# Two of three split-weight tiles get an interleaved layout in a sigmoid-attention and two-FFN kernel

## The chip, the cores and the metric

The kernel runs on one core of a Trainium2 chip. The metric is the device time of one execution in microseconds (us), lower is better. Within the core five engines run side by side and wait for one another through semaphores: TensorE (PE, matrix products; the profile lists its weight loads apart as PEld), VectorE (DVE), ScalarE (ACT), GpSimd (POOL) and SyncE (SP). The last two only issue transfers here.

## The reference

Sigmoid attention over 4 batches, 12 heads, 448 positions and 64 head dimensions is followed by two feed-forward blocks over the 1792 tokens (model width 768, inner width 2048).

```python
scores = scale * np.matmul(q, k.transpose(0, 1, 3, 2)) - np.log(S)
attn = 1.0 / (1.0 + np.exp(-scores))
x = np.matmul(attn, v)              # then to (B * S, H * D)
h = x @ w_in;  g = np.maximum(h, 0) ** 2;       x = g @ w_out      # first block
h = x @ w_in2; g = h / (1 + np.exp(-1.702 * h)); x = g @ w_out2    # second block
```

q, k, v and the output are 32-bit floats. The weights are 64-bit floats and reach the chip as plain bits, which is why the kernel has a step that decodes them.

## The kernel before

**Stages.** Attention comes first. Then come eight stages of the feed-forward blocks (STAGES, line 56): each of the two blocks has its two products, each for two pairs of batches. One product of a stage is done by Strassen's scheme in Winograd's form, so a stage multiplies seven combinations of weight blocks (P1 to P7) with seven combinations of activations, each in NF = 8 steps. One such step is a *unit*; a stage has 56 units and the kernel 448.

**A unit.** Products are done with each 32-bit operand split in a high part, rounded to the type fp32r, and a low part, the rest. A unit covers three chunks of 128 weight columns. For each chunk `product` (line 475) issues three matmuls into one PSUM bank: high weights by high activations (L486), high by low (L487), low by high (L488). Every matmul first loads its 128x128 weights into the array and then streams 448 columns of activations. A unit is nine matmuls, and the 448 units are 4032.

**The weights' way.** `prep` (line 205) decodes the weights, forms the sums that the scheme needs, and stores the blocks to memory. `plan_weights` (line 460) then brings them back for two units at a time (a *pair*; 224 pairs): two transfers fill a tile of LD (four of them, W = 384 columns for each of the two units), ACT writes the high parts to the split tile SL (L470, recorded under the helper's line L164), and DVE subtracts to get the low parts (L472, recorded under L167). There are NSLOT = 3 split tiles, used in turn: pair q has tile q mod 3. ACT may overwrite a tile once the last unit of the pair three before has been multiplied; a unit may start once its pair's low parts are there.

```python
109    SL = [cpool.tile([P, 2, 2, W], F32R, name=f"s{n}") for n in range(NSLOT)]
479            sh, lo = sl[:, 0, unit % 2], sl[:, 1, unit % 2]
484                cols = slice(c * P, (c + 1) * P)
486                nc.tensor.matmul(o, sh[:, cols], t[:, 0, k], start=start, stop=False, skip_group_check=True)
```

So in every partition a split tile has four runs of 384 words, in this order: the high parts of the pair's first unit, those of its second, the low parts of the first, those of the second. Within a run the three chunks of 128 columns follow each other.

**Order.** Instructions are issued in an order that `settle` and `run` work out ahead from planned costs (`act`, `dve`, `move`), which the change leaves as they are. SP issues the LD loads, POOL those of `prep`. The activations' split tiles T, which the matmuls stream, are made by ACT and DVE in `Operand` (line 412) in the same way.

Of the kernel before, what the change touches and what calls it, by code (L numbers as in the profile page):

```python
# [9 lines left out]
F32R = mybir.dt.float32r  # L10
# [8 lines left out]
P = 128  # L19
# [17 lines left out]
NK = 3  # L37
NF = 8
W = NK * P
UNITS = 7 * NF  # L40
NLOAD = 4
NSLOT = 3
# [48 lines left out]
def sigmoid_attention_two_ffn(ctx: ExitStack, tc: tile.TileContext, qk, v, w, outT):  # L91
# [3 lines left out]
    nc = tc.nc  # L95

    def f(ap):
        return ap.bitcast(F32)
# [7 lines left out]
    cpool = ctx.enter_context(tc.tile_pool(name="cpool", bufs=1))  # L106
    X = [[cpool.tile([P, NK, S], F32, name=f"xq{i}{j}") for j in range(2)] for i in range(2)]
    LD = [cpool.tile([P, 2, W], F32, name=f"ld{n}") for n in range(NLOAD)]
    SL = [cpool.tile([P, 2, 2, W], F32R, name=f"s{n}") for n in range(NSLOT)]
    T = []  # L110
    for n in range(NT):
        skip = 0 if n else APART
        t = cpool.tile([P, skip + 2 * NK * S], F32R, name=f"t{n}")
# [34 lines left out]
    def act(fn, n, keys=(), after=(), extra=0.0, **kw):  # L148
        return Node("act", fn, 0.115 + extra + 0.833e-3 * n, keys, after, 0.105, **kw)

    def dve(fn, n, keys=(), after=(), each=1.041e-3, **kw):
        return Node("dve", fn, 0.1 + each * n, keys, after, 0.085, **kw)

    def move(eng, out, in_, size, keys=(), after=(), **kw):

        def go():
            eng.dma_start(out() if callable(out) else out, in_() if callable(in_) else in_)

        n = Node("sp" if eng is nc.sync else "pool", go, 0.45 if eng is nc.sync else 0.55, keys, after, DMA_US + size / 250e3, **kw)
        n.size = size  # L160
        return n

    def activation(out, in_, fn=AF.Copy, **kw):
        nc.scalar.activation(out, in_, fn, **kw)  # L164

    def tt(out, in0, in1, op):
        nc.vector.tensor_tensor(out=out, in0=in0, in1=in1, op=op)  # L167
# [6 lines left out]
    def att_order():  # L174
        for u in range(NHP // 2 + 1):
            if u:
                yield from (("V", hp, c) for hp in (2 * u - 2, 2 * u - 1) for c in range(NFULL))
                yield ("VL", u - 1, 0)
            if u < NHP // 2:
                todo = [("S", hp, c) for hp in (2 * u, 2 * u + 1) for c in range(NFULL)]  # L180
                todo.insert(0 if u else NFULL, ("SL", u, 0))
                yield from todo
# [3 lines left out]
    def make_steps():  # L186
        kind = "L"
        us = {"S": SCORES_US, "V": VALUES_US, "VL": LEFT_US, "SL": LEFT_US}
        for key in att_order():
            new = "L" if key[0] in ("VL", "SL") else key[0]  # L190
            t = us["V" if key in WHOLE else key[0]]
# [61 lines left out]
    def load_qk(hp):  # L253
        if hp > 1:
            n = move(nc.sync, RQ[hp % 4], qk[hp], P * ROW * 4, (), [pe.get(("SL", (hp - 4) // 2, 0)), split.get(hp - 4)], part=0)
            rq_load[hp] = n, n
# [29 lines left out]
    def next_two():  # L286
        turn[0] += 1
        b = 2 * (turn[0] % 4)
        return b, mem["ps"][:, b : b + 2]
# [28 lines left out]
    def scores_left(u):  # L318
        b, ps = next_two()
        step = pe["SL", u, 0]  # L320

# [138 lines left out]
    def plan_weights():  # L460
        for q in range(len(STAGES) * UNITS // 2):
            m, io, _ = STAGES[2 * q // UNITS]
            us = [ORDER[io][(2 * q + i) % UNITS] for i in range(2)]
            t, sl = LD[q % NLOAD], SL[q % NSLOT]
            ld = ("LD", q % NLOAD)
            for i, (p, s) in enumerate(us):
                b = BLOCKS.index(OPERAND[p])
                n = move(nc.sync, t[:, i], scr[m][io][s][:, b], P * W * 4, (), [Node.last.get(ld), scr_ready[m, io, s][b > 3]])
                made["ld", q, i] = n
            hi = act(lambda t=t, sl=sl: activation(sl[:, 0], t), 2 * W, [ld],  # L470
                     [made["ld", q, 0], made["ld", q, 1], units[2 * (q - NSLOT) + 1] if q >= NSLOT else None])
            lo = dve(lambda t=t, sl=sl: tt(sl[:, 1], t, f(sl[:, 0]), ALU.subtract), 2 * W, [ld], [hi])  # L472
            lows.append(lo)

    def product(unit, pairs, ready):
        sl = SL[unit // 2 % NSLOT]

        def go():
            sh, lo = sl[:, 0, unit % 2], sl[:, 1, unit % 2]
            if unit == 0:  # L480
                one = [nc.const_aps.tensor(1.0, [P, n], mybir.dt.bfloat16) for n in (P, D)]
                nc.tensor.matmul(mem["ps"][:, pairs[0][0], :D], *one, start=True, stop=True)  # L482
            for b, c, t, k, start, stop in pairs:
                cols = slice(c * P, (c + 1) * P)
                o = mem["ps"][:, b, :S]
                nc.tensor.matmul(o, sh[:, cols], t[:, 0, k], start=start, stop=False, skip_group_check=True)  # L486
                nc.tensor.matmul(o, sh[:, cols], t[:, 1, k], start=False, stop=False, skip_group_check=True)  # L487
                nc.tensor.matmul(o, lo[:, cols], t[:, 0, k], start=False, stop=stop, skip_group_check=True)  # L488

        units[unit].fn = go  # L490
        units[unit].need(lows[unit // 2], ready)
        for b in {b for b, *_ in pairs}:
            units[unit].need(*held.pop(b, ()))
# [331 lines left out]
    for (i, j), parts in x0parts.items():  # L825
        Node.last["x", i, j] = Node("act", lambda: None, 0.0, (), parts, 0.0)
    plan_weights()
    for st in range(len(STAGES)):
        (plan_out if STAGES[st][1] else plan_in)(st)
# [51 lines left out]
```

## Time and profile before

| what | value |
|---|---|
| median of 2 runs | 941.58 us (940.39 to 942.76) |
| profiled execution, its own time | 939.7 us |
| its span, first to last instruction | 937.9 us |
| PE busy | 933.3 us (100%) |
| PE weight loads busy | 820.9 us (88%) |
| DVE busy | 808.9 us (86%) |
| ACT busy | 604.4 us (64%) |
| granted TensorE clock | 1.0 throughout |

The profile covers one execution. Busy times of matmuls overlap, because the next one starts while the one before still drains, so the pace of PE is read from the starts and not from the durations. A weight load is an instruction of its own on the row PEld and runs beside a matmul. Lines L164 and L167 are those of helpers, so their rows are told apart by the tiles that they name: `s` is a split tile of weights, `ld` what it is made from, `t` a split tile of activations, `raw` and `dec` the weights before and after decoding.

### The profile page before, as it was taken

To read this page: it belongs to the slowest core of one execution; us is meant where nothing else is said; L and a number is where in the kernel's file an instruction comes from. 1 tells how busy PE (TensorE), PEld (TensorE's weight loads), DVE (VectorE), ACT (ScalarE), POOL (GpSimd) and SP (SyncE) were. 2 spreads that over 40 slices of the span, in tenths; PEclk is the share of its full clock that TensorE was granted. 3 is DMA by queue.
4 is the path that set the end of the run, shared out by engine and by line. 5 is a ranking of instruction groups with operands and counts; after the bars stand their busy time and mean duration, and the time that the engine had idled before them with its cause. 6 is when DMAs were issued, how large, how long until landed. Compare 5 with 4: busy or idle time off the path is not lost.

```text
span 937.9 us, 13696 instructions
## 1 busy us (share of the span) xinstructions
PE 933.3 (100%) x4949; PEld 820.9 (88%) x4949; DVE 808.9 (86%) x839; ACT 604.4 (64%) x715; POOL 54.2 (6%) x100
## 2 busy tenths in 40 slices
PE   9999999999999999999999999999999999999998
PEld 4555479999999999999999999999999999999997
DVE  4989986699878999999999997999989999778662
ACT  6788786778868775555464666657684646445551
POOL 0110001010000000000000001000110000000000
PEclk9999999999999999999999999999999999999999
DMA  9899989999897776896478699977975449754341
GB/s 351 296 342 351 343 292 324 334 363 339 287 321 257 245 244 210 303 355 254 160 238 301 196 343 343 329 248 245 356 283 175 134 143 299 268 166 133 118 140 59
DMA packets 98628, 245.93 MB, mean 262 GB/s; under 512 B 10753, under 2 KB 72961, under 8 KB 94465
## 3 DMA queue, kind: packets, MB, share of 16 engines
q1 hardware_dynamic: 84736, 150.70, 47.2%
q0 software_dynamic: 13824, 94.38, 27.6%
q8 instruction: 38, 0.62, 0.3%
q14 instruction: 30, 0.24, 0.1%
HBM read 175.30 MB, written 69.73 MB: 261 GB/s over the span
## 4 chain that ended last, share of the span: by engine, by line
PE 100%; ACT 0%; issue 0%
PE ps L486 29%; PE ps L488 29%; PE ps L487 28%; PE ps L343 6%; PE ps L309 5%; PE ps L357 1%; PE ps L328 1%; PE ps L801 0%; PE ps L304 0%; ACT xq L646 0%; PE ps L482 0%
## 5 line engine op out<-in xcount | busy, mean ns | idle before, releaser
L486 PE MATMUL ps<-t,s 128*128 128x448 f32 x1344 | 488.0, 363 | 0.0
L488 PE MATMUL ps<-t,s 128*128 128x448 f32 x1344 | 487.1, 362 | 0.0
L487 PE MATMUL ps<-t,s 128*128 128x448 f32 x1344 | 483.8, 360 | 0.0
L164 ACT ACTIVATE s<-ld 128x768 fp32r<-128x768 f32 x224 | 189.1, 845 | 240.7 <-PE ps L487 201.2
L488 PEld LDWEIGHTS ps<-t,s 128*128 128x128 f32 x1344 | 252.3, 188 | 19.8
L487 PEld LDWEIGHTS ps<-t,s 128*128 128x128 f32 x1344 | 251.3, 187 | 17.6
L486 PEld LDWEIGHTS ps<-t,s 128*128 128x128 f32 x1344 | 252.4, 188 | 13.0
L167 DVE TENSOR_TENSOR s<-ld,s 128x768 fp32r<-128x768 f32 x224 | 213.6, 954 | 55.8 <-ACT s L164 49.1
L167 DVE TENSOR_TENSOR t<-h,t 128x1344 fp32r<-128x1344 f32 (+1 forms) x72 | 100.5, 1397 | 8.3 <-ACT t L164 8.2
L164 ACT ACTIVATE t<-h 128x1344 fp32r<-128x1344 f32 (+1 forms) x72 | 85.6, 1190 | 4.7 <-DVE h L167 3.2
L164 ACT ACTIVATE h<-ps 128x448 f32<-128x448 f32 x112 | 59.7, 536 | 24.7 <-PE ps L488 24.6
L164 ACT ACTIVATE a<-ps,bias 128x896 f32<-128x896 f32 x72 | 66.2, 1022 | 2.7 <-PE ps L304 2.7
L343 PE MATMUL ps<-a,rv 128*64 128x448 f32 x288 | 56.8, 543 | 0.2
L228 DVE SCALAR_TENSOR_TENSOR dec<-raw,dec 128x1536 uint32<-128x1536 uint32 x32 | 56.2, 1755 | 0.5
L230 DVE SCALAR_TENSOR_TENSOR dec<-raw,dec 128x1536 uint32<-128x1536 uint32 x32 | 56.2, 1755 | 0.3
L164 ACT ACTIVATE dec<-raw 128x1536 f32<-128x1536 f32 x32 | 51.9, 1622 | 0.0
L167 DVE TENSOR_TENSOR h<-h,h 128x1344 f32<-128x1344 f32 (+1 forms) x36 | 50.1, 1397 | 0.6 <-DMA h<-hm 0.4
L164 ACT ACTIVATE h<-h 128x896 f32<-128x896 f32 x48 | 44.9, 947 | 5.1 <-DVE h L167 4.7
L343 PEld LDWEIGHTS ps<-a,rv 128*64 128x64 f32 x288 | 19.6, 137 | 32.5 <-issue 22.6
L224 DVE TENSOR_SCALAR dec<-dec 128x1536 f32<-128x1536 f32 x32 | 30.7, 960 | 15.3 <-ACT dec L164 15.3
L167 DVE TENSOR_TENSOR t<-xq,t 128x1344 fp32r<-128x1344 f32 x24 | 37.2, 1553 | 5.5 <-ACT t L164 5.0
L167 DVE TENSOR_TENSOR h<-ps,h 128x448 f32<-128x448 f32 x64 | 38.8, 620 | 1.8 <-PE ps L488 1.0
(58 smaller groups left out, 616.9 us busy)
## 6 DMA issues: line engine op xcount, KB each, us to landing
ld<-scr SPq DMA_DIRECT2D x448, 192.0 KB, 3.9
raw<-in_w POOLq DMA_DIRECT2D x32, 1536.0 KB, 8.4
scr<-dec POOLq DMA_DIRECT2D x32, 768.0 KB, 5.5
scr<-raw POOLq DMA_DIRECT2D x28, 576.0 KB, 5.9
hm<-h SPq DMA_DIRECT2D x32, 448.0 KB, 5.9
h<-hm SPq DMA_DIRECT2D x16, 672.0 KB, 5.3
rq<-in_qk SPq DMA_DIRECT2D x22, 456.0 KB, 7.9
rv<-in_v SPq DMA_DIRECT2D x12, 448.0 KB, 5.4
```

The costliest lines, as they stand in the source:

```text
L164: nc.scalar.activation(out, in_, fn, **kw)
L167: nc.vector.tensor_tensor(out=out, in0=in0, in1=in1, op=op)
L224: dve(lambda: nc.vector.tensor_scalar(out=d, in0=d, scalar1=LEAST, scalar2=LARGEST, op0=ALU.max, op1=ALU.min), 4 * W, [dk], each=0.52e-3)
L228: dve(lambda: nc.vector.scalar_tensor_tensor(out=u, in0=raw[:, :, 0], scalar=29, in1=u, op0=ALU.logical_shift_right, op1=ALU.bitwise_or), ...
L230: dve(lambda: nc.vector.scalar_tensor_tensor(out=u, in0=raw[:, :, 1], scalar=0x80000000, in1=u, op0=ALU.bitwise_and, op1=ALU.bitwise_or), ...
L309: nc.tensor.matmul(ps[:, j, :S], kk[rows, keys], qq[rows, QUERIES], start=(i == 0), stop=(i == 2))
L328: nc.tensor.matmul(ps[out, j, :S], r[rows, LEFTS], r[rows, QUERIES], start=True, stop=True)
L343: nc.tensor.matmul(ps[rows, :S], t[:, hp % 2 * NFULL + c, rows], a[:, j], start=(c == 0), stop=False)
L357: nc.tensor.matmul(mem["ps"][out, b + i, :S], t[rows, 2 * NFULL, out], AL[rows, j], start=False, stop=True)
L486: nc.tensor.matmul(o, sh[:, cols], t[:, 0, k], start=start, stop=False, skip_group_check=True)
L487: nc.tensor.matmul(o, sh[:, cols], t[:, 1, k], start=False, stop=False, skip_group_check=True)
L488: nc.tensor.matmul(o, lo[:, cols], t[:, 0, k], start=False, stop=stop, skip_group_check=True)
```

## The change

The three split tiles stay the same size and in the same use, but each is now laid out in an order of its own. In the names of the diff, `a` is high or low, `b` the unit of the pair, `k` the chunk, `w` the column within the chunk; the last name is what lies side by side.

- Tile s0 (`a b k w`) is as before.
- Tile s1 (`b k w a`): each word of the high part has its low part beside it. The 128 columns of one chunk, high or low, lie 8 bytes apart.
- Tile s2 (`a b w k`): the same column of the three chunks lies side by side. The 128 columns of one chunk lie 12 bytes apart.

The instructions that write and read the tiles index the same values by the new order. Their number, sizes in elements and waits are the same in the code, and LD, T and the transfers keep their layout.

```diff
-    SL = [cpool.tile([P, 2, 2, W], F32R, name=f"s{n}") for n in range(NSLOT)]
+
+    SL = []
+    for n, order in enumerate(("a b k w", "b k w a", "a b w k")):
+        t = cpool.tile([P, 4 * W], F32R, name=f"s{n}")
+        SL.append(t.rearrange(f"p ({order}) -> p a b k w", a=2, b=2, k=NK))
...
+            t = t.rearrange("p b (k w) -> p b k w", k=NK)
             hi = act(lambda t=t, sl=sl: activation(sl[:, 0], t), 2 * W, [ld],
...
-                cols = slice(c * P, (c + 1) * P)
                 o = mem["ps"][:, b, :S]
-                nc.tensor.matmul(o, sh[:, cols], t[:, 0, k], start=start, stop=False, skip_group_check=True)
-                nc.tensor.matmul(o, sh[:, cols], t[:, 1, k], start=False, stop=False, skip_group_check=True)
-                nc.tensor.matmul(o, lo[:, cols], t[:, 0, k], start=False, stop=stop, skip_group_check=True)
+                nc.tensor.matmul(o, sh[:, c], t[:, 0, k], start=start, stop=False, skip_group_check=True)
+                nc.tensor.matmul(o, sh[:, c], t[:, 1, k], start=False, stop=False, skip_group_check=True)
+                nc.tensor.matmul(o, lo[:, c], t[:, 0, k], start=False, stop=stop, skip_group_check=True)
```

## Rows read from the trace of the kernel before

**Rows 1.** The page, chain that ended last: shares of the span by engine, by line

```profile
PE 100%; ACT 0%; issue 0%
PE ps L486 29%; PE ps L488 29%; PE ps L487 28%; PE ps L343 6%; PE ps L309 5%; PE ps L357 1%; PE ps L328 1%; PE ps L801 0%; PE ps L304 0%; ACT xq L646 0%; PE ps L482 0%
```

**Rows 2.** Instructions on split tiles: count: ns min/median/max, first and last start us

```profile
L486 PEld LDWEIGHTS ps<-t,s x1344: 187/188/201, 127.7 to 933.4; 128*128 128x128 f32 x192
...
L488 PE MATMUL ps<-t,s x1344: 362/362/368, 128.2 to 934.0; 128*128 128x448 f32 x192
L164 ACT ACTIVATE s<-ld x224: 826/846/892, 73.4 to 923.4; 128x768 fp32r<-128x768 f32 x112
L167 DVE TENSOR_TENSOR s<-ld,s x224: 947/953/970, 76.1 to 924.3; 128x768 fp32r<-128x768 f32 x112
```

**Rows 3.** Instructions in order of time, from 299.8 us: start us, us, instruction

```profile
300.03 0.36 PE L486 MATMUL ps<-t,s 128*128 128x448 f32 x1
300.03 0.19 PEld L487 LDWEIGHTS ps<-t,s 128*128 128x128 f32 x1
300.23 0.36 PE L487 MATMUL ps<-t,s 128*128 128x448 f32 x1
300.23 0.19 PEld L488 LDWEIGHTS ps<-t,s 128*128 128x128 f32 x1
```

**Rows 4.** Weight loads in order of time in attention, from 40.4 us

```profile
40.55 0.14 PEld L343 LDWEIGHTS ps<-a,rv 128*64 128x64 f32 x2 [0.23 <-issue]
40.93 0.14 PEld L343 LDWEIGHTS ps<-a,rv 128*64 128x64 f32 x2 [0.23 <-issue]
```

**Rows 5.** Groups by line and form: shape xcount | busy us, mean ns | idle before

```profile
L343 PEld LDWEIGHTS ps<-a,rv 128*64 128x64 f32 x288 | 19.6, 137 | 32.5 <-issue 22.6 <-ACT a L164 9.4 <-ACT s L164 0.5
```

**Rows 6.** Groups by form on ACT: three plain operations and one reading every second word

```profile
L164 ACT ACTIVATE t<-h 128x1344 fp32r<-128x1344 f32 x48 | 63.1, 1315 | 2.3 <-PE ps L488 1.5 <-DVE h L167 0.8
L164 ACT ACTIVATE dec<-raw 128x1536 f32<-128x1536 f32 x32 | 51.9, 1622 | 0.0
L164 ACT ACTIVATE sig<-h 128x896 f32<-128x896 f32 x24 | 22.6, 948 | 2.5 <-DVE h L167 2.1
L164 ACT ACTIVATE t<-h 128x896 fp32r<-128x896 f32 x24 | 22.5, 939 | 2.4 <-DVE h L167 2.3
```

**Rows 7.** Groups by form on DVE: plain, reading every second word (L228), and copies

```profile
L167 DVE TENSOR_TENSOR t<-h,t 128x1344 fp32r<-128x1344 f32 x48 | 74.6, 1554 | 8.3 <-ACT t L164 8.2
L228 DVE SCALAR_TENSOR_TENSOR dec<-raw,dec 128x1536 uint32<-128x1536 uint32 x32 | 56.2, 1755 | 0.5
L167 DVE TENSOR_TENSOR t<-h,t 128x896 fp32r<-128x896 f32 x24 | 26.0, 1084 | 0.0
L272 DVE CAST qh<-rq 128x848 fp32r<-128x848 f32 x22 | 13.2, 600 | 12.8 <-DMA rq<-in_qk 4.6 <-PE ps L343 4.5 <-PE ps L309 3.1
L272 DVE CAST qh<-rq 128x448 fp32r<-128x448 f32 x2 | 0.8, 394 | 3.2 <-DMA rq<-in_qk 3.2
```

**Rows 8.** Instructions in order of time, from 245 us: one pair's split and first load

```profile
246.63 0.85 ACT L164 ACTIVATE s<-ld 128x768 fp32r<-128x768 f32 x1 [0.59 <-PE ps L487]
247.21 0.95 DVE L167 TENSOR_TENSOR s<-ld,s 128x768 fp32r<-128x768 f32 x1
...
250.03 0.19 PEld L486 LDWEIGHTS ps<-t,s 128*128 128x128 f32 x1
```

**Rows 9.** Busy us (and count) by stretch: attention, stage 3, all; granted clock PEclk

```profile
core 0: us, PE busy (x) PEld busy (x) DVE busy (x) ACT busy (x) POOL busy (x), PEclk, DMA share, GB/s
0.00:127.90 127.90, 126.85 (x918) 65.14 (x919) 103.99 (x125) 102.56 (x112) 11.57 (x24) 1.00 0.90 333
...
329.50:430.30 100.80, 100.80 (x506) 94.50 (x505) 98.77 (x93) 59.84 (x62) 3.74 (x7) 1.00 0.82 287
...
sum 934.40, PE 933.35 PEld 820.88 DVE 808.84 ACT 603.89 POOL 54.25; mean PE 103.71 PEld 91.21 DVE 89.87 ACT 67.10 POOL 6.03
```

## Prediction

> **What bounds the kernel now.** I read the chain that ended last first: it is PE from end to end, and 86% of the span lies on the three matmul lines that read the split tiles [rows 1]. No engine and no transfer holds PE up, so the change counts only as far as it alters PE's own pace, or makes another engine so late that PE has to wait.
>
> The second view, the instructions on the split tiles, gives the pace. The L488 matmuls start from 128.2 to 934.0 us, 1344 of them, one in every three [rows 2]: 805.8 / 1343 = 600 ns for three, 200 ns for one. 4032 x 0.2 = 806 us of the 939.7 are that.
>
> What sets the 200 ns? The order of time shows it [rows 3]: a weight load starts together with the matmul ahead of it, takes 188 ns [rows 2], and its own matmul starts some 12 ns after it has ended, when the next load starts too. Loads follow each other with nothing between. [...] Attention has a contrast. There the load has 64 columns and takes 137 ns [rows 5]; the loads come every 377 ns and PEld idles 0.23 us before each [rows 4]. [...] I read the 200 ns as load (188) plus handover (12), not as stream. **So there is no cover over a weight load: each nanosecond that a load becomes longer lengthens the kernel by the same nanosecond.** This is the reading on which the prices below rest.
>
> **The change, part by part.** Nothing is added or removed: the same 224 ACT and 224 DVE operations, the same 4032 loads and matmuls, no new transfer, and no step changes its queue. Pairs go round the three tiles: 75 have s0, 75 have s1, 74 have s2. A pair has 18 loads, so 1350 loads read words 8 bytes apart (s1), 1332 read words 12 bytes apart (s2), and 1350 are as before. The streamed operand t isn't touched.
>
> *Weight loads (the term that matters).* The trace of before has no load with words apart, so I bound it.
> - Of a load's 188 ns, a column takes (188 - 137) / (128 - 64) = 0.8 ns [rows 2, 5], so reading 128 columns takes about 105 ns, at 4 x 128 / 105 = 4.9 bytes per ns; about 83 ns is fixed.
> - Lower end: nothing. What speaks for it is that elsewhere an operation at about one word per 0.8 to 1.0 ns reads every second word at little or no price. DVE: 896 to 1344 elements cost 1084 to 1554 ns, 1.05 a piece, so 1536 plain ones would cost 1554 + 192 x 1.05 = 1755; L228, one of whose inputs has words 8 bytes apart, takes 1755 [rows 7]. No difference.
> - Between: ACT. From 939 at 896 and 1315 at 1344 elements, 0.84 a piece, 1536 plain ones would cost 1476; dec<-raw, 8 bytes apart, takes 1622 [rows 6], 146 more, 0.095 ns an element. (It is another function too, but sig<-h costs 948 where the copy costs 939.) For a load 128 x 0.095 = 12 ns; with both tiles 2682 x 12 = 32 us.
> [...]
> - Upper end: if a load can't sweep more than its own 4.9 bytes per ns, the reading doubles for s1 (+105 ns) and trebles for s2 (+210 ns): 1350 x 0.105 + 1332 x 0.21 = 422 us.
> I take nothing. The nearest rows are strided reads of words at the rate of a weight load; one costs nothing, the other 9%, and both contradict the upper end, under which an 8-byte step would have doubled them. That leaves the 12-byte step, which no row shows.
>
> [...]
>
> *High parts on ACT (L470).* 149 of 224 now write words apart. No row has such a write. Lower end: nothing. Upper end: a write may not sweep faster than now, so its 768 x 0.84 = 645 ns double for s1 (+645 ns) and treble for s2 (+1290 ns). *Low parts on DVE (L472).* They read the high part and write the low one with words apart. Lower end nothing; the copies on DVE write 400 more elements in 600 - 394 = 206 ns [rows 7], 7.8 bytes per ns, at which s1 (768 words, 6144 bytes, 790 ns against 768 x 1.05 = 806) costs nothing and s2 9216 bytes in 1180 ns, +375 ns. The far end, no faster sweep than now, is +806 and +1612 ns. I take nothing for both, because DVE's copies show writes at the rate of s1 and its strided reads cost nothing; s2 stays open to 375 ns.
>
> What hides these? The pairs run ahead of PE. In the tightest pair that I found the low parts are ready at 247.21 + 0.95 = 248.16 and the first load comes at 250.03 [rows 8]: 1.87 us. ACT's far end for s2 with DVE's 375 ns, 1290 + 375 = 1665 ns, still fits once. DVE has less room where it is fullest: in stage 3 it is busy 98.77 of 100.80 us [rows 9]. A stage has 28 pairs, 9.3 of them s2: 9.3 x 0.375 = 3.5 us, where stage 3 has 2.0 idle. PE would then lose a microsecond or two. If this cover is gone, the low parts are late next, then the first load of a unit.
>
> *Waits.* ACT waits to overwrite a tile until the last matmul on its high parts (L487) is done [rows 8]. With high and low interleaved in s1 it may have to wait for L488, 0.2 us later [rows 3]. Behind it in ACT's queue are PSUM evacuations; the cover of 1.87 us holds this too: nothing.
>
> Sum: 0 + 0 + 0 on the profiled execution's 939.7 us. It lies 1.9 us below the median of the two runs, so I forecast that median, 941.6 us.
>
> **The rivals.**
> - *Loads from s2 slow down (slower).* [...] It decides as soon as a load grows by 19 us / 1332 = 14 ns. For it: loads have no cover at all [rows 3], and 12 bytes at 0.83 ns would be a sweep of 14 bytes per ns, which nothing in the trace reaches. Against it: nothing but that strided reads by others were cheap. [...]
> - *A small price on every strided load (slower).* ACT's 0.095 ns an element, 12 ns, on 2682 loads: 941.6 + 32 = 974 us. Against it: DVE paid nothing.
> - *Loads pay in proportion (much slower).* Up to 941.6 + 422 = 1364 us. Against it: both rows of strided reads.
> - *DVE becomes the bound (slower).* Its far end adds 75 x 0.806 + 74 x 1.612 = 180 us. Over the eight stages it is busy 808.84 - 103.99 = 705 of 806.5 us [rows 9], so 885 would be 78 too many: 1020 us if the work spreads evenly, and a few us from stage 3 on where only s2 pays 375 ns. Against it: the copies' 7.8 bytes per ns.
> [...]
>
> **How the numbers follow.** No change of more than 2% (about what a measurement of this kernel can tell from no change, 19 us): 0.54. Loads from s2 slow: 0.25. The small price: 0.08. In proportion: 0.07. DVE: 0.03. Faster: 0.03. That makes slower 0.43, same 0.54, faster 0.03. The likeliest case alone would give 938 to 946. The range reaches to 1020, which takes in the first rival with a little on ACT or DVE, the small price and DVE's bound, and leaves out the proportional case and the faster one; its lower end, 937, is the fastest run less 3 us.
>
> **What would show it.** Weight loads of 188 ns on all three lines, with no second group of durations, and starts 200 ns apart prove the first step. [...] ACT and DVE rows on s with a spread of more than some 30 ns between least and most would show a price for the writes; a wait of PEld for L167 would show that it reaches PE. The forecast is wrong at its root if loads grow and the pace doesn't: then the 200 ns were not the load's.

## The result and the profile after

The changed kernel takes 953.33 us (two runs, 953.13 and 953.52) against 941.58: ratio 1.0134, 95% interval 1.0114 to 1.0153. It is some 12 us slower, clear of noise and below 2%. The 941.58 rests on two runs, 2.4 us apart; 23 later runs of the kernel before have a median of 940.1 us, against which the change would be 13.2 us. The profiled execution takes 953.52 us, its span 951.5.

The instructions on the split tiles come first, as in [rows 2]: count, ns min/median/max, first and last start.

```profile
L490 PEld LDWEIGHTS ps<-t,s x1344: 187/194/255, 127.9 to 947.0; 128*128 128x128 f32 x192
...
L492 PE MATMUL ps<-t,s x1344: 362/367/372, 128.4 to 947.6; 128*128 128x448 f32 x192
L168 ACT ACTIVATE s<-ld x224: 826/922/1342, 73.6 to 936.8; 128x768 fp32r<-128x768 f32 x112
L171 DVE TENSOR_TENSOR s<-ld,s x224: 935/960/1262, 76.3 to 937.7; 128x768 fp32r<-128x768 f32 x112
```

(The lines have moved by four: L490 to L492 are the three matmuls, L168 and L171 ACT's and DVE's helper lines.) Loads, that were 187 to 201 ns, now reach 255; the splits on ACT and DVE have spread too. The matmuls start from 128.4 to 947.6 us: 819.2 / 1343 = 610 ns for three, against 600 before. That is 13.4 us over the stages, nearly all of the 13.6 us by which the span grew (951.5 - 937.9).

Weight loads in order of time show the three tiles. These are the first two loads of a pair of s0, of the next, in s1, and of the third, in s2 (start us, us).

```profile
347.40 0.19 PEld L490 LDWEIGHTS ps<-t,s 128*128 128x128 f32 x1
347.61 0.19 PEld L491 LDWEIGHTS ps<-t,s 128*128 128x128 f32 x1
...
351.01 0.20 PEld L490 LDWEIGHTS ps<-t,s 128*128 128x128 f32 x1
351.21 0.19 PEld L491 LDWEIGHTS ps<-t,s 128*128 128x128 f32 x1
...
354.67 0.25 PEld L490 LDWEIGHTS ps<-t,s 128*128 128x128 f32 x1
354.88 0.26 PEld L491 LDWEIGHTS ps<-t,s 128*128 128x128 f32 x1
```

A pair has 18 matmuls; the pair of s0 takes 351.01 - 347.40 = 3.61 us, that of s1 3.66. Over all pairs of the trace:

| tile (step between words) | mean load, ns | matmul start to start, ns | over the kernel before, all pairs, us | ACT median, ns | DVE median, ns |
|---|---|---|---|---|---|
| s0 (4 bytes) | 187.6 | 200.3 | 0.4 | 848 | 953 |
| s1 (8 bytes) | 194.2 | 203.5 | 4.7 | 922 | 955 |
| s2 (12 bytes) | 252.3 | 206.3 | 8.3 | 1255 | 1225 |

The last row holds the surprise: loads grew by 65 ns, the pace by 6. PE in s2 in order of time shows how:

```profile
355.28 0.37 PE L492 MATMUL ps<-t,s 128*128 128x448 f32 x1
355.29 0.25 PEld L490 LDWEIGHTS ps<-t,s 128*128 128x128 f32 x1
355.49 0.37 PE L490 MATMUL ps<-t,s 128*128 128x448 f32 x1
355.49 0.25 PEld L491 LDWEIGHTS ps<-t,s 128*128 128x128 f32 x1
```

The load for L490 begins at 355.29 and is recorded until 355.54. Its matmul is recorded from 355.49, some 50 ns before, and so is the next load. In [rows 3] the matmul came 12 ns after its load's end.

The splits do not reach PE: the waits list, longest first, has no line in which a weight load on a split tile waited for L168 or L171.

```profile
PEld ps L347 <- issue: 22.8, 98, 0.3
...
PEld ps L347 <- ACT a L168: 9.4, 33, 0.4
PEld ps L361 <- issue: 8.5, 12, 0.7
```

These, PE's largest waits, are all in attention and are as long as before. The tightest pair has its low parts ready 1.67 us before its first load; before it was 1.87 [rows 8].

### The profile page after: what moved, and what is told of

It is laid out like the page before. It is cut to its first block, busy times and chain, and to the rows that moved or that the text cites. A ratio compares the mean times of both kernels' runs of the same rounds, so it can differ in the third digit from the quotient of the medians.

```text
span 951.5 us, 13696 instructions
## 1 busy us (share of the span) xinstructions
PE 946.9 (100%) x4949; PEld 855.6 (90%) x4949; DVE 826.0 (87%) x839; ACT 635.2 (67%) x715; POOL 52.8 (6%) x100
## 4 chain that ended last, share of the span: by engine, by line
PE 99%; DMA 0%; ACT 0%; issue 0%
PE ps L490 29%; PE ps L492 29%; PE ps L491 29%; PE ps L347 6%; PE ps L313 5%; PE ps L361 1%; PE ps L332 1%; DMA rq<-in_qk 0%; PE ps L308 0%; ACT xq L650 0%; PE ps L487 0%
## 5 line engine op out<-in xcount | busy, mean ns | idle before, releaser
L492 PE MATMUL ps<-t,s 128*128 128x448 f32 x1344 | 491.9, 366 | 0.0
L490 PE MATMUL ps<-t,s 128*128 128x448 f32 x1344 | 491.8, 366 | 0.0
L491 PE MATMUL ps<-t,s 128*128 128x448 f32 x1344 | 490.3, 365 | 0.0
L168 ACT ACTIVATE s<-ld 128x768 fp32r<-128x768 f32 x224 | 225.5, 1008 | 223.4 <-PE ps L491 193.1
L492 PEld LDWEIGHTS ps<-t,s 128*128 128x128 f32 x1344 | 283.9, 211 | 10.5
L491 PEld LDWEIGHTS ps<-t,s 128*128 128x128 f32 x1344 | 283.6, 211 | 10.2
L490 PEld LDWEIGHTS ps<-t,s 128*128 128x128 f32 x1344 | 283.9, 211 | 8.5
L171 DVE TENSOR_TENSOR s<-ld,s 128x768 fp32r<-128x768 f32 x224 | 233.9, 1045 | 57.8 <-ACT s L168 56.6
L171 DVE TENSOR_TENSOR t<-h,t 128x1344 fp32r<-128x1344 f32 (+1 forms) x72 | 100.5, 1398 | 6.3 <-ACT t L168 6.3
L168 ACT ACTIVATE t<-h 128x1344 fp32r<-128x1344 f32 (+1 forms) x72 | 85.4, 1188 | 4.6 <-DVE h L171 3.3
L168 ACT ACTIVATE h<-ps 128x448 f32<-128x448 f32 x112 | 59.6, 536 | 21.7 <-PE ps L492 21.4
L168 ACT ACTIVATE a<-ps,bias 128x896 f32<-128x896 f32 x72 | 66.0, 1021 | 3.2 <-PE ps L308 3.2
L168 ACT ACTIVATE dec<-raw 128x1536 f32<-128x1536 f32 x32 | 52.2, 1631 | 0.0
L171 DVE TENSOR_TENSOR h<-h,h 128x1344 f32<-128x1344 f32 (+1 forms) x36 | 50.2, 1401 | 1.5 <-DMA h<-hm 1.4
L168 ACT ACTIVATE h<-h 128x896 f32<-128x896 f32 x48 | 45.0, 947 | 5.5 <-DVE h L171 5.0
L228 DVE TENSOR_SCALAR dec<-dec 128x1536 f32<-128x1536 f32 x32 | 30.8, 962 | 14.1 <-ACT dec L168 14.1
L171 DVE TENSOR_TENSOR t<-xq,t 128x1344 fp32r<-128x1344 f32 x24 | 37.2, 1555 | 4.8 <-ACT t L168 4.8
L161 POOL DMA_DIRECT2D scr<-dec x32 | 17.4, 544 | 410.6 <-DVE dec L171 410.6
```

The lines of the kernel that those rows point to most:

```text
L228: dve(lambda: nc.vector.tensor_scalar(out=d, in0=d, scalar1=LEAST, scalar2=LARGEST, op0=ALU.max, op1=ALU.min), 4 * W, [dk], each=0.52e-3)
L490: nc.tensor.matmul(o, sh[:, c], t[:, 0, k], start=start, stop=False, skip_group_check=True)
L491: nc.tensor.matmul(o, sh[:, c], t[:, 1, k], start=False, stop=False, skip_group_check=True)
L492: nc.tensor.matmul(o, lo[:, c], t[:, 0, k], start=False, stop=stop, skip_group_check=True)
```

## Experiments

**The new code with the old layout.** All three tiles `a b k w`.

```diff
-    for n, order in enumerate(("a b k w", "b k w a", "a b w k")):
+    for n, order in enumerate(("a b k w",) * NSLOT):
```

> The code of the changed kernel with all three tiles in the layout of before. Layout alone is the cause: within 0.2% of the kernel before, loads 188 ns, pitch 200.0 ns. If the new way of writing the accesses costs anything, it shows here.

Measured: 940.42 us, ratio 1.0002 (0.9993 to 1.0011), loads 187.5 ns and pitch 200.0 in all tiles. The layout alone is the cause.

**One changed tile at a time.**

With 8 bytes only:

```diff
-    for n, order in enumerate(("a b k w", "b k w a", "a b w k")):
+    for n, order in enumerate(("a b k w", "b k w a", "a b k w")):
```

> Only tile s1 has the changed layout (8 bytes apart), s0 and s2 are plain. If each tile's price is its own, 75 pairs x 18 matmuls x 3.3 ns = 4.5 us above the kernel before, 0.5%, with loads of 194 ns and pitch 203.5 ns in s1 and 200.0 elsewhere. If the changed code itself costs something apart from the layout, more.

With 12 bytes only:

```diff
-    for n, order in enumerate(("a b k w", "b k w a", "a b w k")):
+    for n, order in enumerate(("a b k w", "a b k w", "a b w k")):
```

> Only tile s2 has the changed layout (12 bytes apart), s0 and s1 are plain. 74 pairs x 18 x 6.3 ns = 8.4 us above the kernel before, 0.9%, with loads of 252 ns and pitch 206.3 ns in s2 alone; the two parts then add up to the whole change (12 to 13 us). If the prices were not each tile's own, the sum would differ.

Measured: 8 bytes alone 944.94 us, ratio 1.0051 (1.0038 to 1.0063), 4.8 us; the changed tile has loads of 194.0 ns and pitch 203.1. 12 bytes alone 949.99 us, ratio 1.0104 (1.0089 to 1.0119), 9.9 us; loads 252.1, pitch 206.3. The first came as expected. The second is 1.5 us dearer than expected; in its profile the matmuls of s2 are 8.3 us late, the last matmuls of the pairs ahead of them 0.6, and the stretch after the last matmul is 5.5 us where it is 3.9 before, which no layout explains. The sum, 14.7, lies above the whole change's 12, within the intervals. In the traces the pairs are 4.5 and 8.9 us longer than before in sum, which makes the 13.4 of the whole change. Each tile has a price of its own.

**All tiles at 12 bytes.**

```diff
+    for n, order in enumerate(("a b w k",) * NSLOT):
```

> All three tiles in the layout with 12 bytes between words. Stream plus handover: 4032 x 6.25 ns = 25 us, 967 us, if the longer splits on ACT (1250 ns) and DVE (1220 ns) stay hidden. DVE then needs 98.8 + 28 x 0.267 = 106.3 us in stage 3, which lasts 104, so if its cover is as thin as it looks a few us more, and PE waits for L171 in stages 3 and 4. Prediction's theory (load of 252 ns sets the pace): 1200 us.

Measured: 967.39 us, ratio 1.0289 (1.0272 to 1.0307); 4032 x 6.25 ns had given 967. All splits are long now, ACT's 1267 and DVE's 1230 ns. Stretches of stage length, the third and fourth, show how full that makes DVE (columns as in [rows 9]).

```profile
336.30:440.50 104.20, 104.20 (x506) 104.20 (x506) 103.92 (x91) 69.97 (x62) 3.72 (x7) 1.00 0.79 272
440.50:544.70 104.20, 104.20 (x506) 104.20 (x505) 103.82 (x92) 66.88 (x56) 5.48 (x10) 1.00 0.62 211
```

DVE is busy 103.92 of 104.20 us, and PE is busy throughout; the 106.3 that had been expected did not all fall into this stretch, in which DVE has 91 instructions where it had 93 [rows 9]. One pair in the seventh stage lasts 0.7 us longer than the others. There PE did wait for DVE, for the low part of an activations' tile that stood behind two weight splits in DVE's order:

```profile
803.83 0.25 PEld L491 LDWEIGHTS ps<-t,s 128*128 128x128 f32 x1 [0.65 <-DVE t L171]
```

In the same pair the weights' low parts were ready only 0.1 us after its first load had started. So the cover just held for three times the price of the change.

**Short streams.** The second matmul of each three streams fewer columns.

```diff
-                nc.tensor.matmul(o, sh[:, c], t[:, 1, k], start=False, ...)
+                n = 384 - 64 * c
+                nc.tensor.matmul(o[:, :n], sh[:, c], t[:, 1, k, :n], start=False, ...)
```

> The layouts of the changed kernel, but the second of the three matmuls (high weights by low activations) streams only 384, 320 or 256 columns in the first, second and third chunk; the rest of that term is left out. Prediction's theory (the load sets the pace, nothing covers it): in plain tile s0 the start after a short stream still comes 200 ns later, and the time stays at 953 us. Stream plus handover: 173, 147 and 120 ns in s0, with 3 and 6 ns more in s1 and s2 until the load itself, which in s2 took 252 ns, gets in the way; 448 x 160 ns = 72 us less if the other engines keep up, 880 to 900 us.

Measured: 911.99 us, above the 880 to 900 expected. (This kernel and those below were run once each; what is read from them is the pace of the tiles within one trace.) PE in order of time in a pair of s0 (here L492 is the short matmul, L493 the third):

```profile
335.29 0.28 PE L492 MATMUL ps<-t,s 128*128 128x256 f32 x1
335.30 0.19 PEld L493 LDWEIGHTS ps<-t,s 128*128 128x128 f32 x1
335.41 0.36 PE L493 MATMUL ps<-t,s 128*128 128x448 f32 x1
335.41 0.19 PEld L490 LDWEIGHTS ps<-t,s 128*128 128x128 f32 x1
335.60 0.36 PE L490 MATMUL ps<-t,s 128*128 128x448 f32 x1
```

A stream of 256 columns is followed after 0.12 us, while the load for the next matmul still has 80 ns of its record to go. Median starts after 384, 320 and 256 columns are 173, 145 and 113 to 118 ns in s0; the author's estimate had been 173, 147 and 120. Each 64 columns fewer bring the start 27 to 29 ns forward, 0.42 to 0.45 ns a column, at which 448 columns are 188 to 202 ns of the 200.3; what is left for a handover these medians don't settle. **The pace goes with the stream; plain loads are covered.** In s2 the same starts come after 175 to 180, 143 to 148 and 120 to 122 ns, but after 320 and 256 columns what follows is late: 148 + 231, 120 + 264 and 122 + 253 ns. In order of time the matmul after the short one starts 0.12 us behind it, the next 0.27 us later still:

```profile
341.98 0.28 PE L492 MATMUL ps<-t,s 128*128 128x256 f32 x1
342.10 0.42 PE L493 MATMUL ps<-t,s 128*128 128x448 f32 x1
342.37 0.37 PE L490 MATMUL ps<-t,s 128*128 128x448 f32 x1
```

Two loads there need some 380 ns together, 190 each, whichever stream was short. So, as an estimate from these sums, a load recorded as 252 ns holds up what follows for about 190, and the pitch of 206 ns under streams of 448 columns hides that with 16 ns to spare. In s0 two starts come as close as 320 ns, so a plain load needs at most 160. The saving is smaller than the 72 us expected because of these catch-ups (some 9 us) and because weight loads now waited for other engines (some 19 us, of which 10.8 for the low parts, in 18 cases).

**Half loads.** The third matmul loads 64 columns.

```diff
-                nc.tensor.matmul(o, lo[:, c], t[:, 0, k], start=False, stop=stop, ...)
+                nc.tensor.matmul(o[: P // 2], lo[:, c, : P // 2], t[:, 0, k], start=False, stop=stop, ...)
```

> The layouts of the changed kernel, but the third matmul of each three loads only 64 of the 128 columns of the low weights; the low-by-high term of the other half of the output rows is left out. Prediction's theory (pitch is load plus 12 ns): in plain tile s0 this load takes 137 ns and its matmul starts as soon as the stream allows, 187 to 190 ns after the one ahead, so three take 588 to 590 ns in place of 600. Stream plus a handover that does not depend on the load's length: 600 ns in s0 still, and the 609 and 619 of three in s1 and s2 stay. If it is the reading of the load beside the stream that slows the stream, s1 and s2 lose about a sixth of their excess of 10 and 20 ns in three.

Measured: 954.04 us. A triple of s0 in order of time:

```profile
349.18 0.36 PE L491 MATMUL ps<-t,s 128*128 128x448 f32 x1
349.19 0.14 PEld L492 LDWEIGHTS ps<-t,s 128*64 128x64 f32 x1
349.38 0.36 PE L492 MATMUL ps<-t,s 128*64 128x448 f32 x1
349.39 0.19 PEld L490 LDWEIGHTS ps<-t,s 128*128 128x128 f32 x1
349.58 0.36 PE L490 MATMUL ps<-t,s 128*128 128x448 f32 x1
```

The load takes 0.14 us, the matmul still starts 0.20 after the one ahead. Three take 602 ns in s0, 612 in s1, 617 in s2: a load some 54 ns shorter gains nothing. The 187 to 190 ns expected of the stream were the author's estimate.

**Quarter loads.** Second and third matmul load 32 columns.

```diff
+                nc.tensor.matmul(o[: P // 4], sh[:, c, : P // 4], t[:, 1, k], start=False, ...)
+                nc.tensor.matmul(o[: P // 4], lo[:, c, : P // 4], t[:, 0, k], start=False, ...)
```

> The layouts of the changed kernel, but the second and third matmul of each three load only 32 of the 128 columns of weights; high-by-low and low-by-high terms of the other 96 output rows are left out. Prediction's theory (pitch is load plus 12 ns): the two short loads cost no more than the stream, three matmuls in plain tile s0 take about 575 ns in place of 600. A handover that doesn't depend on the load's length: 600 ns in s0. For the excess of three matmuls in s1 and s2 (10 and 20 ns in the changed kernel): if reading the load beside the stream slows the stream word by word, half the words are left and the excess halves, to 5 and 10 ns (605 and 610); if it sits at the head or the end of each load, 10 and 20 stay (610 and 620).

Measured: 954.55 us; three take 613 ns in s0, 610 in s1, 609 in s2. In s0 in order of time:

```profile
348.72 0.37 PE L490 MATMUL ps<-t,s 128*128 128x448 f32 x1
348.72 0.11 PEld L491 LDWEIGHTS ps<-t,s 128*32 128x32 f32 x1
348.92 0.36 PE L491 MATMUL ps<-t,s 128*32 128x448 f32 x1
348.93 0.11 PEld L492 LDWEIGHTS ps<-t,s 128*32 128x32 f32 x1
349.13 0.37 PE L492 MATMUL ps<-t,s 128*32 128x448 f32 x1
```

None of the theories gives this. Loads of 108 ns made the plain tile *slower*, by 4.1 ns a matmul against the changed kernel's s0, and the excess of the wide steps over the plain tile is gone. So the handover does not shrink with the load's length, nor does it simply follow the words read beside the stream.

**High or low parts alone at 12 bytes.**

```diff
+    for n, orders in enumerate((("b k w", "b k w"), ("b k w", "b w k"), ("b w k", "b k w"))):
+        t = cpool.tile([P, 4 * W], F32R, name=f"s{n}")
+        SL.append([t[:, 2 * W * a : 2 * W * (a + 1)].rearrange(f"p ({o}) -> p b k w", b=2, k=NK) for a, o in enumerate(orders)])
```

> In tile s1 only the low parts are 12 bytes apart, in s2 only the high parts, s0 is plain. If a matmul's own load sets its handover, in s1 one start in three is late by some 6 ns (75 x 6 x 6.25 ns = 2.8 us) and in s2 two in three (74 x 12 x 6.25 ns = 5.6 us): about 950 us. If it were something of the tile as a whole, all would be late in both. ACT writes only the high parts: 845 ns in s0 and s1, about 1250 in s2. DVE reads high and writes low: if the read is what costs 267 ns, s2 shows it and s1 does not; if the write, the other way round.

Measured: 951.81 us. The handover again is not each load's own: three matmuls take 613 to 614 ns both with one wide load in three (s1) and with two (s2), where three wide ones take 619. A change of kind between neighbouring loads may cost as well. The quarter loads would fit that, the half loads do not (602 ns in s0); it is not shown.

For DVE it is plain. Splits of three pairs running, of s0, s1 and s2:

```profile
342.38 0.97 DVE L171 TENSOR_TENSOR s<-ld,s 128x768 fp32r<-128x768 f32 x1
346.19 1.21 DVE L171 TENSOR_TENSOR s<-ld,s 128x768 fp32r<-128x768 f32 x1
348.72 1.20 DVE L171 TENSOR_TENSOR s<-ld,s 128x768 fp32r<-128x768 f32 x1
```

Writing 12 bytes apart (second) and reading 12 bytes apart (third) cost the same, 1.21 us each, and both together 1.23 (s2 of the changed kernel, 1225 ns). Here the read and the write of one instruction don't add up.

**Wider steps: 16, 24 and 48 bytes.**

```diff
+    for n, order in enumerate(("k w a b", "a w b k", "w a b k")):
```

> The three split tiles get layouts in which the 128 columns of a load lie 16, 24 and 48 bytes apart. Theory A (stream plus a handover that grows with the step): from tile s0 to s2 of the changed kernel the pitch of matmuls was 200.3, 203.5 and 206.3 ns at 4, 8 and 12 bytes, so about 3.2 ns for each further 4 bytes: 210, 216 and 235 ns, about 1025 us in all. Theory B (only the number of 16-byte groups that a load's words fall into counts): beyond 16 bytes every word has its own, so all three tiles have the same pitch, whatever it is. Theory C (the prediction's: pitch is load plus 12 ns): pitch follows the load's duration one to one in every tile.

Measured: 1119.97 us. Instructions on the split tiles:

```profile
L490 PEld LDWEIGHTS ps<-t,s x1344: 310/330/373, 128.6 to 1113.5; 128*128 128x128 f32 x192
...
L168 ACT ACTIVATE s<-ld x224: 1601/1658/1770, 74.3 to 1101.2; 128x768 fp32r<-128x768 f32 x112
L171 DVE TENSOR_TENSOR s<-ld,s x224: 1559/1620/1811, 77.0 to 1102.9; 128x768 fp32r<-128x768 f32 x112
```

By tile the pitch is 235, 230 and 268 ns, loads 332, 326 and 371. Theory A fails (230 at 24 bytes is below 235 at 16), and so does C (loads and pitch stand 96 to 103 ns apart, not -12). B holds roughly up to 24 bytes, not at 48. The stream is the same 448 columns, and the pitch now follows the load, 96 to 103 ns below its record in each tile: from 16 bytes on it is the load that sets the pace. Whether it does so alone, or load and stream also hinder each other, no run shows. No weight load on a split tile waited for ACT or DVE here either.

The same steps order what ACT and DVE pay. Taking off each engine's fixed part (200 ns on ACT, 150 on DVE, from 845 and 954 at 768 elements and 0.84 and 1.05 ns apiece [rows 6, 7]):

| step, bytes | 16-byte groups touched per word | ACT, ns per word | DVE, ns per word | PE, ns per word |
|---|---|---|---|---|
| 4 | 0.25 | 0.84 | 1.05 | about 0.8 |
| 8 | 0.5 | 0.94 | 1.05 | hidden |
| 12 | 0.75 | 1.37 | 1.40 | 1.5 (190 / 128) |
| 16 | 1 | 1.88 | 1.91 | 1.84 (pitch / 128) |
| 24 | 1 | 1.98 | 2.03 | 1.80 |
| 48 | 1 | 1.88 | 1.89 | 2.10 |

One number fits nearly all of it: about 1.87 ns for each 16-byte group that an access touches, beside the engine's own pace; the slower of the two counts. 0.5 x 1.87 = 0.94 exceeds ACT's 0.84 and not DVE's 1.05; 0.75 x 1.87 = 1.40 exceeds both. It fits the strided read in the kernel before, too: dec<-raw [rows 6], (1622 - 200) / 1536 = 0.93 on ACT, and no loss on DVE [rows 7]. This is a fit over these runs, and for PE from 16 bytes on it divides the pitch, not a measured reading time. PE's 1.5 at 12 bytes lies a little above the fit's 1.40; at 48 bytes PE has another price, which stays open.

## Why the prediction was right or wrong

*The forecast of no change beyond 2%, and the range, held; the likeliest case did not.* It was to give 938 to 946 us, and the kernel took 953.33. It is slower by 1.3%. The place is one that the prediction named, the loads of words apart, but the time is not in the loads' own length, and no row of before could give its size. That the forecast held is luck: two errors, told below, offset each other.

*What sets the 200 ns: wrong, and the root of it.* The prediction read load plus 12 ns, since in [rows 3] each matmul started just after its load had ended. Two things that end together looked like cause and effect. Three runs contradict it: loads of 252 ns with starts 206 apart, a matmul 120 ns after a short stream while its load of 188 ns went on, and half loads that left 200 ns as they were. Load records overlap at 12 bytes: each starts a few ns after a matmul's start, whether or not the record of the load ahead is over. What the pace goes with is the stream: 0.42 to 0.45 ns a column in the run with short streams, 188 to 202 ns for 448 columns. How much of the 200 ns is a handover, no run shows. The prediction said what would show this: loads that grow and a pace that doesn't. The contrast in [rows 4, 5] tells nothing of it. Its rows say x2: each 377 ns hold two loads and two matmuls, recorded some 6 ns apart. So they give no pace of one matmul after one load. A short load alone doesn't bring the next start forward, as the half loads show (602 ns for three).

*"There is no cover over a weight load": wrong.* The cover is the stream. Loads of 4 and 8 bytes and, with 16 ns to spare, of 12 bytes fit under it; at 16 bytes they don't, and then the pitch is 230 ns and more.

*The price of a load: wrong, in the other direction.* "I take nothing" met 6.7 ns at 8 bytes and 64.8 at 12. Had there been no cover, as the prediction had it, the loads as measured would have made the time 1350 x 6.7 + 1332 x 64.8 ns = 95 us longer, about 1037. The two errors offset each other: loads did slow down as the rival had it, and nearly all of it was hidden.

*The rivals.* Loads from s2 slow down: right on the load (64.8 ns longer), wrong on the time. No run shows the price at which the range, up to 1020 us, takes it in; in its place the runs showed 8.3 us for s2. The small price on every strided load (12 ns, 32 us) comes nearest in size: 3.5 and 6.3 ns, 13 us; its cause was not the one given. The proportional case and DVE as the bound did not come.

*Sweep as the measure: right only in part.* The bounds for loads, ACT and DVE counted the bytes that an access sweeps; a rate of about 16 / 1.87 = 8.6 bytes per ns fits up to 16 bytes of step. Beyond, the number of 16-byte groups counts and not the distance: ACT at 24 and 48 bytes pays about what it pays at 16 (1.98 and 1.88 ns per word against 1.88).

*ACT and DVE: taken as nothing, in fact inside the bounds.* s2 cost ACT 409 ns (bounds 0 and 1290) and DVE 270 (0 and 375); s1 cost ACT some 80 and DVE nothing. That all this is hidden was right. The prediction feared for DVE in stage 3, because it is nearly always busy there; the run with all tiles at 12 bytes filled it to 103.92 of 104.20 us there, and PE waited for it once, 0.65 us, in another stage. A busy share near 100% was not yet a bound.

*What stays open.* Why starts under the same stream of 448 columns come 200.3, 203.5 and 206.3 ns apart as the step grows: that the layout causes it is shown, by what mechanism is not. It isn't simply each load's own price. In s1, where all loads are alike, starts mostly come 200 and 207 ns apart in turn, and in s2 203 and 210 (medians by place in the pair). Open too is why loads of 32 columns cost the plain tile 4 ns a matmul and loads of 64 columns 0.3. Neither the load's length nor the number of words read beside the stream explains the runs.

## What to carry to other kernels

That a matmul starts just as its load ends doesn't prove that it waits for it: shorten the stream, or the load, and see which of them moves the start. Weights 8 or 12 bytes apart cost 3.5 and 6.3 ns a matmul here under a stream of 448 columns; from 16 bytes on the load set the pace (230 to 268 ns), and at 12 bytes it did where two matmuls would otherwise have started within less than some 380 ns. Count the 16-byte groups that an access touches, at about 1.9 ns each by the fit over these runs, and compare with the engine's own pace (0.84 ns per word on ACT, 1.05 on DVE); on DVE the read and the write of one instruction didn't add up (1.21 us each, 1.23 both).

## What the runs showed of the hardware

- A matmul's record can start before its own load's record has ended, by 50 ns at 12 bytes (changed kernel) and by about 80 after a short stream of a plain tile (short streams). At 12 bytes load records overlap each other: 252 ns long, 206 ns apart.
- One price per 16-byte group, about 1.87 ns by a fit over these runs, fits ACT, DVE and, by the pitch, weight loads (1.80 to 2.03 at steps of 16 bytes and more, but 2.10 for PE at 48).
- Shorter loads can slow the matmuls: with two loads of 32 columns in three, the plain tile went from 200.3 to 204.4 ns a matmul.
